# Score copies behind state updates, a plain output for the second block, block sums on VectorE, and rounding spread over the first turns

## Chip, cores, metric

One core of one Trainium2 chip. The metric is the device time of one execution in microseconds (us); "span" is the time between the first and the last instruction in a profiled execution, some 1.7 to 2.0 us less. All executions reported here were in the fast state, so all of them can be compared.

## The reference, cut

```python
def _attn_ref(q, k, v, f_logit):            # (4, 8, 768, 48): batch, heads, tokens, head_dim
    f = 1.0 / (1.0 + np.exp(-f_logit))
    state = np.zeros((B, H, D, D)); y = np.zeros_like(q)
    for t in range(S):
        state = f[:, :, t, :, None] * state + np.einsum('bhd,bhe->bhde', k[:, :, t], v[:, :, t])
        y[:, :, t] = np.einsum('bhd,bhde->bhe', q[:, :, t], state)
    return y

def _moe_ref(x, w_in, w_out):               # 3072 x 384, 384 x 2048, 2048 x 384
    h = x @ w_in
    sp = np.maximum(h, 0.0) + np.log1p(np.exp(-np.abs(h)))
    return (h * erf(sp)) @ w_out
# reference = _moe_ref(x = attention's y as 3072 rows of 384, w_in, w_out)
```

The linear attention runs in 24 chunks of 128 tokens. The weights and the other inputs arrive as 64-bit numbers, which the kernel turns into float32 on the chip; this work on the weights is what "rounding" means below.

## The kernel before, where the change touches it

A chunk passes through stages d (decays: matmul, two exponentials on ScalarE, two multiplies on VectorE), t (transposes), s (scores and state) and y (attention's output). The two engines concerned meet in d and in s:

```python
    def stage_d(g):
        ...
        nc.tensor.matmul(ps, lhsT=tri[:], rhs=lts[blk][:, j, :], start=True, stop=True)
        nc.scalar.activation(out=dp[:, :, 0:D], in_=..., func=AF.Exp, scale=-1.0)
        nc.scalar.activation(out=kd, in_=..., func=AF.Exp)
        ...
        nc.vector.tensor_tensor(out=qd[:, :, 0:D], in0=..., in1=dp[:, :, 0:D], op=ALU.mult)   # waits for ScalarE
        nc.vector.tensor_tensor(out=kd, in0=..., in1=kd, op=ALU.mult)

    def stage_s(g):
        ...   # matmuls into one PSUM tile of two banks: sc (scores), dS (state increments)
        for c in range(2):
            for r in range(2):
                if FIRST <= g < 2 * ADJACENT:          # chunks 3 to 9
                    nc.scalar.copy(out=qA[half(1 - r), r, :, half(c)], in_=sc[half(c), r])
                    ...                                 # causal mask on GpSimd
                    continue
                nc.vector.tensor_tensor(...)            # the other chunks: VectorE copies and masks
        next_state(2 * g, dS)                           # VectorE: 4 small instructions, 2 of them read dS
        if not last:
            late[g] = lambda: next_state(2 * g + 1, dS)  # 4 more, at the next stage t or at y
```

The slots of a turn, in which everything else is placed (cut):

```python
            for s, _ in enumerate(gen):                 # one matmul group of PE per slot
                due += (1 if s < 42 else 0.6 if s < 72 else 0.3) if it == 0 else 0.42 if it == 1 else 0.6
                while due >= 1:
                    weights_step(); due -= 1            # one rounding step, on VectorE
                if at and s == at[0]:
                    ...                                 # a stage of a chunk
                if it + 3 < n_blocks and s == prepare_at:
                    prepare(it + 3, 0, CPB)             # VectorE clamps the gate logits, ScalarE exp, ln
                ...
                if step:
                    act_step()                          # a step of h * erf(softplus(h)), ScalarE and VectorE by turns
                ...
                    sum_step()                          # additions for the block-wise output product
```

The output product is either plain (8 x 4 products of blocks) or block-wise with 7 products in place of 8, which needs sums of blocks of w_out (`sum_w`, 16 additions, on GpSimd) and of the activations, and additions of the results.

## Time and profile before

| | before |
|---|---|
| median of the runs first given | 628.98 us (3 runs, 628.93 to 629.83) |
| span of the profiled run | 627.6 us |
| busy: PE, VectorE (DVE), ScalarE (ACT), GpSimd (POOL) | 94, 75, 61, 6% |
| first hidden matmul, end of turns 0, 1, 2, 3 | 28.2, 105.5, 134.6, 192.4, 250.3 us |
| end of turn 3 to the end of the span | 377.3 us |

The view of instruction groups for 28 to 250 us gives one more reading that matters later. A line holds the operation, its count, after the bar its busy time and the mean ns of one, then the idle time of its engine just before these instructions and what ended it:

```profile
L438 DVE TENSOR_TENSOR sv<-sc,sv 48x192 f32<-48x192 f32 x36 | 12.8, 355 | 7.6 <-ACT qA L488 6.9
...
L488 ACT COPY qA<-sc 64x256 f32<-64x256 f32 x28 | 10.3, 367 | 3.3 <-PE sc L468 2.8
```

VectorE stood 7.6 us before state updates, 6.9 of it for ScalarE's score copies; ScalarE stood only 3.3 us before these copies. The change sets out to remove the first number.

### The profile page before, as it was taken

What the parts mean: (1) busy time and instruction counts of PE and PEld (TensorE: products, weight loads), DVE (VectorE), ACT (ScalarE), POOL (GpSimd) and SP (SyncE); (2) the same over time, 40 slices, a digit from 0 to 9 for tenths busy, and PEclk for the clock granted to TensorE, in tenths of its full rate; (3) what the DMA queues carried; (4) which work ended last, traced back from release to release, by engine and by line L of the source; (5) the groups of instructions that cost most, each with busy time, mean ns of one, the idle gap of its engine ahead of it and who ended that gap; (6) DMA issues with size and microseconds to landing.
All of it is one profiled execution on the core that took longest, in us unless ns stands there. A gap on an engine that the chain in (4) does not pass through costs nothing.

```text
span 627.6 us, 13891 instructions
## 1 busy us (share of the span) xinstructions
PE 589.5 (94%) x5777; PEld 524.7 (84%) x5777; DVE 470.2 (75%) x788; ACT 382.4 (61%) x483; POOL 38.4 (6%) x49
## 2 busy tenths in 40 slices
PE   8788699998976999999999999999999999999995
PEld 7567588887644988988998998998998989989995
DVE  4998998695589778678787876797887694756751
ACT  5725457978864457756675776765775656556200
POOL 1000011010176000000000000000000000000000
PEclk9879799999989899999999999999999999999999
DMA  9997743440321043043052052052030000000000
GB/s 200 247 241 215 216 123 63 88 78 12 63 56 26 1 78 76 1 79 75 4 102 52 2 102 51 3 102 52 3 76 14 2 27 1 19 8 1 25 26 29
DMA packets 155587, 41.35 MB, mean 66 GB/s; under 512 B 147328, under 2 KB 150400, under 8 KB 155520
## 3 DMA queue, kind: packets, MB, share of 16 engines
q1 hardware_dynamic: 153440, 40.02, 29.3%
q8 instruction: 47, 0.77, 0.5%
q10 hardware_dynamic: 2080, 0.39, 0.3%
q14 instruction: 20, 0.16, 0.1%
HBM read 35.59 MB, written 4.72 MB: 64 GB/s over the span
## 4 chain that ended last, share of the span: by engine, by line
PE 72%; DVE 12%; issue 6%; ACT 5%; DMA 2%; SPq 1%; POOL 1%; DVEq 0%; ACTq 0%; POOLq 0%
PE ops L717 31%; PE hps L587 29%; PE y L525 3%; PE ps_t L411 2%; PE ops L670 2%; PE ps_d L380 2%; DVE sv L438 1%; PE sc L460 1%; PE sc L468 1%; DVE sv L439 1%; DVE w_in_sb L322 1%; DMA qn<-in_q_dram 1%; DVE qA L496 1%; DVE w_in_sb L336 1%; ACT L160 1%
## 5 line engine op out<-in xcount | busy, mean ns | idle before, releaser
L587 PE MATMUL hps<-xT,w_in_sb 128*128 128x256 f32 x1152 | 264.7, 386 | 7.8 <-DVE w_in_sb L336 4.4
L587 PEld LDWEIGHTS hps<-xT,w_in_sb 128*128 128x128 f32 x1152 | 218.2, 192 | 41.2 <-DVE w_in_sb L336 3.4
L165 DVE SCALAR_TENSOR_TENSOR e<-x,e 128x1024 f32<-128x1024 f32 x96 | 120.2, 1252 | 13.5 <-ACT x L160 13.2
L160 ACT ACTIVATE x<-Hg,serf_bias 128x1024 f32<-128x1024 f32 x88 | 97.6, 1141 | 0.2
L157 ACT ACTIVATE e<-Hg 128x1024 f32<-128x1024 f32 x44 | 46.6, 1058 | 77.0 <-DVE Hg L561 73.2
L717 PE MATMUL ops<-wT,Hg 128*128 128x192 f32 x352 | 87.6, 331 | 0.0
L717 PE MATMUL ops<-wT,scratch 128*128 128x192 f32 x320 | 76.5, 331 | 5.9 <-DVE scratch L615 5.9
L717 PE MATMUL ops<-w_out_sb,Hg 128*128 128x192 f32 x352 | 72.6, 329 | 0.0
L561 DVE TENSOR_TENSOR Hg<-Hg,e 128x1024 f32<-128x1024 f32 x44 | 54.6, 1240 | 22.5 <-ACT e L559 22.4
L717 PEld LDWEIGHTS ops<-wT,Hg 128*128 128x128 f32 x352 | 62.1, 192 | 2.2
L594 ACT COPY Hg<-hps 128x1024 f32<-128x1024 f32 x44 | 44.4, 1010 | 31.0 <-PE hps L587 30.7
L717 PEld LDWEIGHTS ops<-w_out_sb,Hg 128*128 128x128 f32 x352 | 60.7, 192 | 2.6
L717 PEld LDWEIGHTS ops<-wT,scratch 128*128 128x128 f32 x320 | 57.0, 193 | 6.2 <-issue 6.2
L559 ACT ACTIVATE e<-e 128x1024 f32<-128x1024 f32 x48 | 50.4, 1050 | 6.4 <-DVE e L165 6.3
L496 DVE TENSOR_TENSOR qA<-sc,tri 64x256 f32<-64x256 f32 x68 | 28.7, 422 | 22.3 <-PE sc L468 21.3
L725 DVE TENSOR_TENSOR scratch<-scratch,ops 128x384 f32<-128x384 f32 (+1 forms) x44 | 22.2, 504 | 30.3 <-ACT scratch L733 25.0
L418 ACT COPY qA<-ps_t 64x512 f32<-64x512 f32 x48 | 27.7, 578 | 22.5 <-PE ps_t L411 20.6
L395 DVE TENSOR_TENSOR qd<-qn,dp 128x384 f32<-128x384 f32 x24 | 13.4, 556 | 35.6 <-ACT dp L383 34.4
L717 PE MATMUL ops<-w_out_sb,scratch 128*128 128x192 f32 x160 | 39.5, 328 | 0.0
L525 PEld LDWEIGHTS y<-qA,sv 128*32 128x32 f32 x1536 | 24.6, 113 | 17.2 <-issue 9.2
L525 PE MATMUL y<-qA,sv 128*32 128x64 f32 x1536 | 28.9, 226 | 9.3 <-issue 6.9
L438 DVE TENSOR_TENSOR sv<-sc,sv 48x192 f32<-48x192 f32 x80 | 28.4, 354 | 8.3 <-ACT qA L488 6.9
(109 smaller groups left out, 648.9 us busy)
## 6 DMA issues: line engine op xcount, KB each, us to landing
lt<-in_f_logit_dram SPq DMA_DIRECT2D x24, 192.0 KB, 3.8
qn<-in_q_dram SPq DMA_DIRECT2D x24, 192.0 KB, 3.3
out_dram<-scratch SPq DMA_DIRECT2D x12, 384.0 KB, 2.6
kn<-in_k_dram SPq DMA_DIRECT2D x23, 192.0 KB, 3.5
vt<-in_v_dram SPq DMA_DIRECT2D x23, 192.0 KB, 3.6
sv<-in_v_dram SPq DMA_DIRECT2D x84, 48.0 KB, 2.9
w_out_sb<-in_moe_w_in_dram SPq DMA_DIRECT2D x4, 768.0 KB, 6.3
Hg<-in_moe_w_in_dram SPq DMA_DIRECT2D x4, 768.0 KB, 6.4
```

What stands on the lines that cost most here:

```text
L157: nc.scalar.activation(out=dst[:], in_=h, func=AF.Exp)
L160: nc.scalar.activation(out=dst[:], in_=h, func=AF.Tanh, bias=serf_bias[:, i : i + 1], scale=SERF_KAB[i][0])
L165: nc.vector.scalar_tensor_tensor(out=e[:], in0=x[:], scalar=SERF_KAB[i][2], in1=e[:], op0=ALU.add, op1=ALU.mult)
L418: nc.scalar.copy(out=qAs[g][half(r), r], in_=pss[0][half(r)])
L438: nc.vector.tensor_tensor(out=new, in0=add, in1=old, op=ALU.add)
L496: nc.vector.tensor_tensor(out=qA[half(1 - r), r, :, half(c)], in0=sc[half(c), r], in1=tri1[half(c)].unsqueeze(1).broadcast_to((C, HP, C)), ...
L525: nc.tensor.matmul(y[M * i : M * (i + 1), kt, half(c)], lhsT=sv[:, r, c, a, o : o + M], rhs=qA[:, r, a, half(c)], start=(n == 0), stop=Tru ...
L559: nc.scalar.activation(out=e[:], in_=e[:], func=AF.Tanh, scale=SERF_C)
L561: nc.vector.tensor_tensor(out=h, in0=h, in1=e[:], op=ALU.mult)
L587: nc.tensor.matmul(hps[:, j, :], lhsT=w_in_sb[:, kt, ft * P : (ft + 1) * P], rhs=xTs[blk][:, kt, :], start=(kt == 0), stop=(kt == n_k - 1),)
L594: nc.scalar.copy(out=gr["h"], in_=hps[:])
L717: nc.tensor.matmul(place[n], lhsT=x[:, j, :], rhs=y, start=(gi == 0 and j == 0 and n in first), stop=(gi == n_g - 1 and j == 1), skip_grou ...
```

## The change

Its intent: take VectorE's waits and bunches out of the first turns. Chunks 3 to 9 update the state *before* ScalarE copies the scores. Block 1 gets the plain output product (as block 0 had), so that its sums and additions go. The sums of w_out move from GpSimd to VectorE, and are placed one to every second slot. Rounding and activation steps get a more even pace; the first pieces of the weights are loaded and rounded earlier. The core of the diff:

```diff
+        by_scalar = FIRST <= g < 2 * ADJACENT
+        if by_scalar:
+            next_state(2 * g, dS)
         for c in range(2):
             for r in range(2):
-                if FIRST <= g < 2 * ADJACENT:
+                if by_scalar:
                     nc.scalar.copy(out=qA[half(1 - r), r, :, half(c)], in_=sc[half(c), r])
@@
-        next_state(2 * g, dS)
+        if not by_scalar:
+            next_state(2 * g, dS)
@@ sum_w, four times
-        add(t[:, 0], b12, b11, ALU.subtract, nc.gpsimd)
+        add(t[:, 0], b12, b11, ALU.subtract)
@@ slots(it)
+        if it == 3:
+            return chain(project_first(1), *hiddens(4)), n_ft * CPB + n_h
@@ loads at the start
-        load(1, "qk")
+        load_piece(0)
+        load(1, "qkv")
+        load_piece(1)
         load_f(2)
-        load_piece(0)
-        load(1, "v")
         load(2)
-        load_piece(1)
@@
         stage_t(0)
+        weights_steps(2)
@@ turn 0's places for stages
-                at = [1, 5, 6, 12, 16, 23, 34, 42, 48, 52, 60, 74, 76, 80, 88, 94]
+                at = [1, 5, 8, 12, 16, 23, 36, 43, 48, 52, 60, 74, 76, 80, 88, 94]
@@ rounding
-                due += (1 if s < 42 else 0.6 if s < 72 else 0.3) if it == 0 else 0.42 if it == 1 else 0.6
+                due += (1 if s < 18 else 0.46 if s < 66 else 0.3) if it == 0 else 0.45
@@ activations
-                if it < 2:
-                    step = it == 1 and s % 6 == 3
-                elif it == 2:
-                    step = s % 5 in (1, 3)
+                if it == 0:
+                    step = s >= 24 and s % 8 == 5
+                elif it == 1:
+                    step = s % 5 == 3
+                elif it < 4:
+                    step = s % 7 in (1, 4)
+                elif it == n_blocks - 1:
+                    step = s % 3 == 1
@@ sums
-                    if s == n - 6:
-                        to_sum.extend(sum_h(groups[1, gi]) for gi in range(NS))
-                    sum_step()
+                    if s % 2:
+                        sum_step()
```

(Cut: the places of the sums in memory, the pace of the sums in turn 3, chunk places of turn 2, a prepare ten slots later.)

More of the change, by code (lines that the diff above doesn't have):

```diff
@@ L602, in places @@
         own = [[sums_sb[:, b, n] for n in range(NA)] for b in range(NS)]
-        for _ in range((n_blocks - 3) * n_g // NS):
+        for _ in range((n_blocks - 4) * n_g // NS):
             yield from own
@@ L607, in places @@
             own.insert(0, [x[:, 0 : S_WORDS // (NS * NA)].rearrange("p (j t) -> p j t", j=FG // 2) for x in t])
-        own = own[1::-1] + own[3:] + own[2:3]
+        own = own[1::-1] + own[2:]
         while True:
@@ L612, with add @@
     sum_places = places()
-    def add(out, x, y, op=ALU.add, engine=nc.vector):
-        engine.tensor_tensor(out=out, in0=x, in1=y, op=op)
+    def add(out, x, y, op=ALU.add):
+        nc.vector.tensor_tensor(out=out, in0=x, in1=y, op=op)
     def sum_w(gi):
@@ L621, in sum_w @@
         t = w_sums(gi)
-        add(t[:, 0], b12, b11, ALU.subtract, nc.gpsimd)
+        add(t[:, 0], b12, b11, ALU.subtract)
         yield
-        add(t[:, 1], b22, t[:, 0], ALU.subtract, nc.gpsimd)
+        add(t[:, 1], b22, t[:, 0], ALU.subtract)
         yield
-        add(t[:, 2], b22, b12, ALU.subtract, nc.gpsimd)
+        add(t[:, 2], b22, b12, ALU.subtract)
         yield
-        add(t[:, 3], b21, t[:, 1], ALU.subtract, nc.gpsimd)
+        add(t[:, 3], b21, t[:, 1], ALU.subtract)
     def blocks(h):
@@ L676, in project_first @@
                     if j == FG - 1 and tt == CPB - 1:
-                        to_sum.append(sum_w(gi))
+                        if blk == 0:
+                            to_sum.append(sum_w(gi))
                         if gi == n_g - 1:
@@ L912 @@
             if it == 0:
-                todo = [(stage_s, 2), (stage_y, 2), (stage_d, 3), (stage_t, 3), (stage_s, 3), (stage_y, 3),
+                todo = [(stage_s, 2), (stage_d, 3), (stage_y, 2), (stage_t, 3), (stage_s, 3), (stage_y, 3),
                         (stage_d, 4), (stage_t, 4), (stage_d, 5), (stage_s, 4), (stage_t, 5),
                         (stage_y, 4)] + stages(2)[4:]
-                at = [1, 5, 6, 12, 16, 23, 34, 42, 48, 52, 60, 74, 76, 80, 88, 94]
+                at = [1, 5, 8, 12, 16, 23, 36, 43, 48, 52, 60, 74, 76, 80, 88, 94]
             else:
@@ L920 @@
             if ADJACENT <= it + 2 < n_blocks:
-                at = ([0] if it + 2 == ADJACENT else []) + [2, 26, 42, 54, 76, 90]
+                at = [0, 1, 15, 24, 31, 52, 66] if it + 2 == ADJACENT else [2, 26, 42, 54, 76, 90]
                 at = at[: len(todo)]
@@ L944 @@
                             load_piece(7)
-                if it == 0 and s == 14:
+                if it == 0 and s == 24:
                     prepare(2, 0, CPB)
@@ L963 @@
                 if it == 2:
-                    if s == n - 6:
-                        to_sum.extend(sum_h(groups[1, gi]) for gi in range(NS))
-                    sum_step()
+                    if s % 2:
+                        sum_step()
                 elif it > 2:
-                    if s == n_o and it < n_blocks - 1:
+                    if s == n - n_h and it < n_blocks - 1:
                         to_sum.extend(sum_h(groups[it - 1, gi]) for gi in range(NS))
@@ L972 @@
                         to_sum.extend(sum_h(groups[blk, gi]) for gi in range(NS))
-                    if s < n_o or s % 3 == 0 or it == n_blocks - 1:
+                    if it == 3:
+                        if s % 2:
+                            sum_step()
+                    elif s < n_o or s % 3 == 0 or it == n_blocks - 1:
                         sum_step()
```

## The prediction

> **Names.** The kernel runs twelve turns, one per block of 256 tokens. A turn is a list of slots; one slot is one hidden matmul (L587) or one output matmul (L670, L717). Between slots the program puts attention stages (d, t, s, y of a chunk), rounding steps for the weights (16 pieces of 6 steps, 96 in all) and activation steps (10 per group, a new group every 5). This order fixes what each in-order engine does next.
>
> **What bounds the kernel now.** First the page, parts 1 and 2:
>
> ```profile
> PE 589.5 (94%) x5777; PEld 524.7 (84%) x5777; DVE 470.2 (75%) x788; ACT 382.4 (61%) x483; POOL 38.4 (6%) x49
> ...
> PE   8788699998976999999999999999999999999995
> ...
> POOL 1000011010176000000000000000000000000000
> PEclk9879799999989899999999999999999999999999
> ```
>
> One digit is 15.7 us. PE idles, and its clock drops, only before about 220 us, so only the first turns can give much. I counted hidden matmuls in PE's timeline to find where turns 0 to 5 begin and end, and asked for the windows of these stretches (busy PE, PEld, DVE, ACT, POOL, then granted clock, DMA share, GB/s):
>
> ```profile
> 28.20:105.50 77.30, 67.00 (x736) 55.00 (x736) 71.86 (x119) 36.59 (x60) 5.80 (x8) 0.87 0.70 178
> 105.50:134.60 29.10, 28.69 (x372) 23.88 (x371) 21.68 (x37) 27.04 (x39) 3.15 (x4) 1.00 0.42 72
> 134.60:192.40 57.80, 51.92 (x439) 37.82 (x439) 41.38 (x49) 42.44 (x52) 19.50 (x16) 0.97 0.27 48
> 192.40:250.30 57.90, 50.94 (x533) 46.07 (x532) 47.69 (x80) 33.51 (x39) 6.91 (x7) 0.94 0.24 48
> 250.30:298.10 47.80, 46.82 (x486) 42.57 (x486) 35.77 (x64) 32.78 (x38) 0.00 (x0) 1.00 0.27 52
> 298.10:344.50 46.40, 46.40 (x487) 42.50 (x486) 36.93 (x65) 30.95 (x36) 0.00 (x0) 1.00 0.28 53
> ```
>
> Turn 0 is VectorE's: 72 of 77 us busy, and nearly every piece of the chain between 12 and 72 us is a VectorE instruction, most of them rounding. Turn 5 is the undisturbed kernel, PE without a gap. Turns 2 and 3 carry PE holes beside GpSimd's work. PE's waits name the holes:
>
> ```profile
> PE y L525 <- issue: 6.9, 4, 3.8
> PE ops L717 <- DVE scratch L615: 5.9, 1, 5.9
> PE ps_t L411 <- DVE qd L395: 5.6, 1, 5.6
> PE hps L587 <- DVE w_in_sb L336: 4.4, 2, 3.0
> ```
>
> Last, VectorE's timeline around GpSimd's block sums (172 to 199 us), the same kind of addition during them and after:
>
> ```profile
> 197.95 1.21 DVE L615 TENSOR_TENSOR scratch<-Hg 128x256 f32<-128x256 f32 x1
> ...
> 204.50 0.42 DVE L615 TENSOR_TENSOR scratch<-Hg 128x256 f32<-128x256 f32 x1
> ```
>
> **What the Trainium skill says.** (1) "SBUF — State Buffer", section "Who interferes with whom": a VectorE instruction with two SBUF inputs and a GpSimd instruction that reads SBUF exclude each other for a whole instruction. The trace agrees: 0.42 us becomes 1.21 us. (2) "PSUM — Partial Sum Buffer", section "PSUM bank collisions raise a hardware error": two engines in one bank have to be ordered by software, reads included. The trace agrees: state updates (L438) wait for ScalarE's score copies (L488), 8.6 us in 4 waits, although both only read the score tile. (3) "TensorE: Matmul & The Clock Gate", Part 1: an idle window of about 3.4 us halves PE's clock, and it comes back after about as long a busy one. The trace agrees roughly: after the 5.6 us hole at 66.6 us the clock is 0.55 in 72 to 76 us, and after the hole that ends at 203 us pairs of output matmuls run at 0.64 us in place of 0.325. So a hole of 5 us costs near 7.
>
> **The change part by part.**
>
> *Plain output for block 1.* From the chain: 32 L717 records take 5.20 us, so 0.1625 each (a float32 matmul is two records). Block-wise: 56 x 2 x 0.1625 = 18.2 us. Plain: 32 matmuls of twice the columns, an estimate of 32 x 2 x 0.325 = 20.8 us. PE pays **+2.6 us**. In return, block 1's 16 additions (16 x 0.43 = 6.9 us of VectorE) and 4 evictions (2.2 us) go, and with them the 5.9 us wait on its sums at the start of turn 3.
>
> *Block sums of w_out on VectorE.* 16 additions of 128x384 at about 0.55 us (the duration of L395, same shape): +8.8 us of VectorE. Gone is the mutual exclusion: adding up what VectorE's instructions from 172 to 199 us take beyond their usual durations gives about 9.7 us. A wash in busy time, but it is spread over turns 2 and 3, and the mask for y of chunk 8 no longer queues behind these sums (the 3.8 us hole that ends at 178 us).
>
> *Rounding spread.* Six steps of a piece take 0.56 + 0.56 + 0.96 + 0.56 + 0.96 + 0.96 = 4.55 us, 0.79 a step with gaps. When qd of chunk 4 is due, the old order has emitted 10 + 35 = 45 steps, the new one 12 + 18 + 0.46 x 19 = 38 or 39: 6.5 x 0.79 = 5 us less VectorE work in front of it. In turn 0 this is path: the 5.6 us hole ends by that qd.
>
> *Loads and the start.* Piece 0 now comes ahead of chunk 1's loads and its first steps ahead of d of chunk 1. At the 220 GB/s of the first windows piece 0 lands near 10 us; f of chunk 2 comes behind two pieces, near 15 us. I count 1 to 2 us of new stalls, mostly regained as the rounding is further on: the first hidden matmul at 29.5 instead of 28.3.
>
> *State updates first.* VectorE loses 8.6 us of waiting, but ScalarE's copies now wait for a VectorE that is behind. For y of chunk 3 I work out copies at 54.9 to 56.4 us (before: 52.6 to 54.2), so this y comes 1 us later than before, with a hole in front of it.
>
> *Turn 0* then: slot 24 near 59 us (before 57.5), t of chunk 4 near 67.5 without a wait (before 72.2, then half clock), the rest limited by PE as before: **it ends near 99.8 instead of 105.5.**
>
> *Turn 1*: VectorE gets 21.6 steps x 0.79 = 17, attention 9 and activations 7 = 33 us against 28 of PE. From 55 us to the end of turn 2 I sum 53 (rounding) + 30 (attention) + 27 (activations) + 6 (sums) = 116 us of VectorE in some 122: 95%. It keeps up, barely, and I allow 1 us here and 1.5 in turn 2. Turn 1 takes 29, ending at 128.8.
>
> *Turn 2*: 96 hidden records 20.7 (from the chain), plain 20.8, stages 7 (turn 5: 46.4 - 18.2 - 20.7 = 7.5) = 48.5, with the allowance 49.7, ending at **178.5 (before 192.4)**. Activations are further on (33 steps when the first plain output starts, 10 needed), so no forced bunch.
>
> *Turn 3*: 20.8 + 20.7 + 8 (one more s) = 49.5, with waits 50: **228.5 (before 250.3)**. Turn 4 stays at 47.8, and from 298.1 to the end 329.5 us stay as they are, since PE has no gap there. Sum: 228.5 + 47.8 + 329.5 = 605.8 us of span; the median before is 1.4 us over its span, so **607 us**.
>
> **The rivals.**
> *VectorE is the bound and stays it.* It was 93% busy in turn 0; total work hardly falls. Holes would move from t of chunk 4 into turns 1 and 2, where rounding now lies beside activations. For it: the 95% above, with dependency stalls of some 5% seen between 72 and 144 us. Against: turn 1 before had 7 us free. Then the end of turn 2 is at 184 or later: 612 to 618 us.
> *ScalarE becomes hostage to VectorE.* Copies of scores wait for updates at the end of VectorE's queue, and evictions of hidden groups queue behind them; two buffers give 5 us of grace. Each such wait costs PE up to 4 us and the clock. For it: y of chunk 3 above. Against: from turn 1 VectorE is hardly behind. 610 to 615 us.
> *The start slips.* Moved loads stall d of chunk 1 and the prepare of chunk 2 by more than I count: up to +4 us, 611 us.
> *All holes close.* Turns 0 to 3 at their content: turn 0 near 95, then 28, 48 and 49: 598 us.
>
> **Range and chances.** The holes of turns 2 and 3 (5.9 and 3.8 us, plus the half clock behind each, plus contention) have causes that the diff plainly removes: 10 to 15 us after paying 2.6. Turn 0 gives 3 to 10. The 2% line is at 616.4, a gain of 12.6; only if turn 0 gives nothing and turns 1 and 2 show new holes is it missed. Predicted 607 us, 80% range 600 to 616; faster by over 2%: 0.87, within: 0.11, slower: 0.02.
>
> **What would show it right or wrong.** Right: PE's waits without L717 on L615 and without the 5.6 us on qd; no GpSimd sums, L615 at 0.42 to 0.55 us throughout; VectorE no longer waiting for L488; turn boundaries near 100, 129, 178 and 228; turn 5 at 46.4. Wrong: new PE waits on qd, state or masks in turns 1 and 2 with VectorE over 95% busy there (first rival); ScalarE waiting for L438 or L439 by many us with PE waiting for L594 (second); the first hidden matmul after 32 us (third); or a steady turn other than 46.4.

## The result

628.69 us median of 4 runs (627.44 to 629.04) against 629.17 us of before (4 runs, 628.93 to 629.83). The ratio is 0.9987 with a 95% interval of 0.997 to 1.0004: no change. Ratios here are the mean time of one kernel's fast runs over that of the other's of the same rounds, so not quite the ratio of the medians quoted. I had predicted 607 and gave "within 2%" a chance of 0.11.

The page of the changed kernel, parts 1 and 2 (busy time per engine; then digits per slice of 15.7 us):

```profile
PE 591.9 (94%) x5729; PEld 517.7 (83%) x5729; DVE 461.2 (74%) x784; ACT 384.6 (61%) x485; POOL 16.6 (3%) x33
...
PE   7695999879899999999999999999999999999995
...
POOL 1001011100100000000000000000000000000000
PEclk9978899898999999999999999999999999999998
```

GpSimd has lost its sums, as intended. PE's gaps have moved to the left: slices 4, 8 and 9 (47 to 63 us, 110 to 141 us) where before the largest lay at 63 to 78 us and at 173 to 204 us. The windows of turns 0 to 5 (stretch, length, then busy PE, PEld, DVE, ACT, POOL, granted clock, DMA share, GB/s):

```profile
29.70:105.30 75.60, 67.93 (x736) 55.21 (x736) 62.89 (x104) 44.89 (x67) 6.56 (x8) 0.87 0.68 179
105.30:145.90 40.60, 32.87 (x372) 27.21 (x372) 30.17 (x47) 27.16 (x40) 3.39 (x4) 0.87 0.33 57
145.90:199.00 53.10, 50.08 (x440) 36.61 (x439) 42.93 (x65) 36.74 (x47) 3.41 (x4) 1.00 0.27 48
199.00:249.00 50.00, 50.00 (x486) 37.18 (x485) 38.22 (x65) 37.04 (x42) 0.51 (x2) 1.00 0.26 53
249.00:295.50 46.50, 46.50 (x486) 42.59 (x485) 37.46 (x66) 30.63 (x36) 0.00 (x0) 1.00 0.28 53
295.50:341.90 46.40, 46.40 (x486) 42.50 (x485) 37.23 (x66) 32.85 (x39) 0.00 (x0) 1.00 0.28 53
```

Turn 1 is the surprise: 40.6 us where before took 29.1 and I predicted 29.0. In turns 0 and 1 the granted clock is 0.87. Turns 2 to 4 gain 4.7, 7.9 and 1.3 us; turn 0 gains 1.7 in place of 7; turn 1 loses 11.5. That is where the gain went: not hidden, but spent again in turn 1 and at the start (1.5 us). PE's waits:

```profile
PE y L528 <- POOL qA L493: 8.5, 3, 4.3
PE y L528 <- issue: 6.3, 4, 3.1
...
PE ps_t L411 <- DVE qd L395: 0.8, 1, 0.8
```

The waits that were predicted to go are gone (5.9 us on the block sums; qd fell from 5.6 to 0.8). New ones hold y, the product that needs the copied and masked scores. The groups in 28 to 250 us, to be laid beside those of before:

```profile
L438 DVE TENSOR_TENSOR sv<-sc,sv 48x192 f32<-48x192 f32 x37 | 13.1, 355 | 2.0 <-ACT qA L490 1.2
...
L490 ACT COPY qA<-sc 64x256 f32<-64x256 f32 x28 | 10.3, 367 | 26.6 <-DVE sv L438 11.6 <-DVE sv L439 8.2 <-DVE sv L436 5.3
```

VectorE's wait fell from 7.6 to 2.0 us. ScalarE's, before the same 28 copies, rose from 3.3 to 26.6. How one of these waits comes about is seen in the three engines' timelines of turn 1 (start, duration, instruction, in brackets the idle time before it and what ended it). ScalarE:

```profile
130.06 0.51 ACT L383 ACTIVATE dp<-ps_d 128x384 f32<-128x384 f32 x1
130.43 0.52 ACT L386 ACTIVATE kd<-ps_d 128x384 f32<-128x384 f32 x1
136.21 1.51 ACT L490 COPY qA<-sc 64x256 f32<-64x256 f32 x4 [5.26 <-DVE sv L438]
...
140.37 1.02 ACT L597 COPY Hg<-hps 128x1024 f32<-128x1024 f32 x1
```

VectorE in the same stretch:

```profile
130.60 0.56 DVE L395 TENSOR_TENSOR qd<-qn,dp 128x384 f32<-128x384 f32 x1 [2.39 <-ACT dp L383]
131.07 0.55 DVE L399 TENSOR_TENSOR kd<-kn,kd 128x384 f32<-128x384 f32 x1
...
132.61 1.22 DVE L564 TENSOR_TENSOR wT<-wT,e 128x1024 f32<-128x1024 f32 x1
133.74 1.22 DVE L165 SCALAR_TENSOR_TENSOR e<-x,e 128x1024 f32<-128x1024 f32 x1
134.99 0.35 DVE L438 TENSOR_TENSOR sv<-sc,sv 48x192 f32<-48x192 f32 x1
```

And PE:

```profile
139.97 1.30 PE L528 MATMUL y<-qA,sv 128*32 128x64 f32 x38 [3.73 <-POOL qA L493]
```

Read it as a chain. VectorE stands at qd until ScalarE's exponential dp is there (2.39 us). Both engines then go on together, but ScalarE's next instructions are the score copies, and these may not read the tile until VectorE's state updates have. VectorE has six other instructions queued ahead of those (qd, kd, two rounding steps, two activation steps), 4.4 us from 130.60 to 134.99. So ScalarE stands for 5.26 us, and everything behind the copies comes later: the mask on GpSimd, then in ScalarE's own queue the transposes' copies and the eviction of a hidden group at 140.37. PE runs out and waits 3.73 us at y. Then VectorE in turn arrives early at the next qd: its waits for dp in 55 to 199 us are 21.0 us in the changed kernel, 4.8 us (55 to 192 us) before. Two in-order queues stand for each other by turns. The Trainium skill, "TensorE: Matmul & The Clock Gate", in its table at the top and Part 1, calls the queues of ScalarE and VectorE strict first-in, first-out; the trace agrees: nothing in ScalarE's queue ran in those 5.26 us, although PE had finished at 133.2 us the transposes that ScalarE was to copy.

Chunk by chunk (3 to 9), ScalarE's waits before these copies are 8.2, 3.4, 0, 5.3, 5.3, 3.0 and 1.2 us, so the chain above, chunk 7's, is not the only case. The longest, chunk 3's, comes about otherwise: VectorE waits for nobody there, but works off rounding steps without a gap from 47.7 to 53.9 us before it gets to the updates. There it is late by its load.

### The profile page after: what moved, and what is told of

Read it like the earlier page. It is cut to its first block, busy times and chain, and to the rows that moved or that the text cites. A ratio compares the mean times of both kernels' runs of the same rounds, so it can differ in the third digit from the quotient of the medians.

```text
span 627.3 us, 13755 instructions
## 1 busy us (share of the span) xinstructions
PE 591.9 (94%) x5729; PEld 517.7 (83%) x5729; DVE 461.2 (74%) x784; ACT 384.6 (61%) x485; POOL 16.6 (3%) x33
## 4 chain that ended last, share of the span: by engine, by line
PE 71%; DVE 12%; ACT 7%; SPq 3%; DMA 3%; issue 2%; POOL 0%; ACTq 0%; DVEq 0%
PE hps L590 30%; PE ops L721 25%; PE ops L673 7%; PE y L528 3%; PE ps_t L411 2%; PE ps_d L380 2%; DVE sv L438 1%; PE sc L468 1%; PE sc L460 1%; ACT x L160 1%; SPq L391 1%; DVE sv L439 1%; DVE qA L498 1%; DVE Hg L564 1%; DVE e L165 1%
## 5 line engine op out<-in xcount | busy, mean ns | idle before, releaser
L590 PE MATMUL hps<-xT,w_in_sb 128*128 128x256 f32 x1152 | 269.5, 391 | 5.6 <-ACT xT L532 2.0
L590 PEld LDWEIGHTS hps<-xT,w_in_sb 128*128 128x128 f32 x1152 | 221.5, 195 | 41.2 <-ACT xT L532 2.8
L165 DVE SCALAR_TENSOR_TENSOR e<-x,e 128x1024 f32<-128x1024 f32 x96 | 117.1, 1220 | 17.0 <-ACT x L160 16.5
L721 PE MATMUL ops<-wT,Hg 128*128 128x192 f32 x320 | 78.9, 328 | 0.0
L721 PE MATMUL ops<-wT,scratch 128*128 128x192 f32 x288 | 67.8, 326 | 0.9 <-DVE scratch L729 0.9
L721 PE MATMUL ops<-w_out_sb,Hg 128*128 128x192 f32 x320 | 65.1, 326 | 0.0
L721 PEld LDWEIGHTS ops<-wT,Hg 128*128 128x128 f32 x320 | 55.8, 190 | 1.9
L721 PEld LDWEIGHTS ops<-w_out_sb,Hg 128*128 128x128 f32 x320 | 54.6, 190 | 2.0
L721 PEld LDWEIGHTS ops<-wT,scratch 128*128 128x128 f32 x288 | 50.3, 190 | 1.1 <-issue 1.1
L498 DVE TENSOR_TENSOR qA<-sc,tri 64x256 f32<-64x256 f32 x68 | 28.7, 422 | 28.3 <-PE sc L468 27.4
L721 PE MATMUL ops<-w_out_sb,scratch 128*128 128x192 f32 x144 | 35.2, 326 | 0.0
```

The costliest lines, as they stand in the source:

```text
L165: nc.vector.scalar_tensor_tensor(out=e[:], in0=x[:], scalar=SERF_KAB[i][2], in1=e[:], op0=ALU.add, op1=ALU.mult)
L498: nc.vector.tensor_tensor(out=qA[half(1 - r), r, :, half(c)], in0=sc[half(c), r], in1=tri1[half(c)].unsqueeze(1).broadcast_to((C, HP, C)), ...
L590: nc.tensor.matmul(hps[:, j, :], lhsT=w_in_sb[:, kt, ft * P : (ft + 1) * P], rhs=xTs[blk][:, kt, :], start=(kt == 0), stop=(kt == n_k - 1),)
L721: nc.tensor.matmul(place[n], lhsT=x[:, j, :], rhs=y, start=(gi == 0 and j == 0 and n in first), stop=(gi == n_g - 1 and j == 1), skip_grou ...
```

## The experiments

15 kernels, all correct within the tolerance. Theory: the swap of state updates and score copies ate the gain. Rivals: VectorE's amount of work, the activation pace, the new start. Against the kernel before, only runs 13 and 15 are faster by a clear 2%; runs 7, 9 and 12 lie at that line.

### 1. The changed kernel, swap undone

```diff
-        if by_scalar:
-            next_state(2 * g, dS)
...
-        if not by_scalar:
-            next_state(2 * g, dS)
+        next_state(2 * g, dS)
```

> The changed kernel with one part undone: state updates again behind ScalarE's score copies. Theory A (ScalarE held by VectorE): in the changed kernel ScalarE stood 25 us in turns 0 and 1 waiting for state updates (8.2 + 3.4 + 5.3 + 5.3 + 3.0), and PE lost 11.6 us in turn 1 on the masks behind those copies. With the order undone turn 1 falls from 40.6 to about 30 us and the time to 612 to 618 us. Theory B (turn 1 has too much VectorE work, whatever the order): turn 1 stays at 38 us or more, VectorE waits for ScalarE in place of the reverse, time 625 to 630 us.

618.98 us (617.82 to 619.16, 4 runs), ratio to before 0.9836 (0.9817 to 0.9856), span 616.1. Against the changed kernel this is 9.7 us; it lies 1 us above the range of theory A (612 to 618) and far from that of B. The same place of the program in ScalarE's timeline:

```profile
121.83 0.50 ACT L386 ACTIVATE kd<-ps_d 128x384 f32<-128x384 f32 x1
122.36 1.52 ACT L488 COPY qA<-sc 64x256 f32<-64x256 f32 x4
```

The copies follow the exponentials at once; VectorE's row of instructions from qd to the state update is even longer than in the changed kernel (5.3 us, 121.99 to 127.28) and does not hold up the copies. Turn 0 ends at 99.5 us, as predicted (99.8). Turns 1 and 2 take 32.3 and 55.8 us, 9.4 us more than predicted, turn 3 takes 50.0 as predicted. So the swap is one half of the miss, and something in turns 1 and 2 is the other.

### 2. The kernel before, swap alone

```diff
+        if by_scalar:
+            next_state(2 * g, dS)
         ...                                   # copies
-        next_state(2 * g, dS)
+        if not by_scalar:
+            next_state(2 * g, dS)
```

> The kernel before with only the swap: state updates ahead of the score copies. Theory A: VectorE is most behind in turn 0 here (93% busy), so ScalarE is held at chunks 3 to 7 and the time rises by 3 to 12 us, to 632 to 641 us. Theory B: the swap by itself is neutral or a small gain (8.6 us of VectorE waits gone), 624 to 630 us.

630.71 us (629.22 to 633.34, 20 runs), ratio 1.0025 (1.0013 to 1.0036). It costs 1.5 us here, in place of the 9.7 us in the changed kernel; the time lies between the ranges of the two theories. ScalarE stands before the copies of chunks 3 to 9 here too (1.0, 6.9, 4.0, 1.8, 3.1, 0 and 1.2 us), so its waits do not turn into time one for one. PE's y waits appear here as well (3.2 us on the mask at 55 us, 2.1 at 133 us), and turn 2 ends 3 us later than before, but at 205 us the wait on GpSimd's block sums has shrunk (5.2 us for 5.9). That this wait takes up a part of the loss is argued, not shown; why turn 1 itself loses less here is open (run 4 points to the old activation pace, which this kernel has).

### 3. The changed kernel, score tile split in two

The tile of two banks becomes two tiles of one bank, so that state updates and copies order each other bank by bank; two copies go ahead, then the update, then two copies.

```diff
-        ps = ps_sc.tile([P, 2, 512], FP32, name="sc", tag="sc")
+        pss = [ps_sc.tile([P, 512], FP32, name=f"sc{i}", tag=f"sc{i}") for i in range(2)]
@@
-        if by_scalar:
-            next_state(2 * g, dS)
-        for c in range(2):
-            for r in range(2):
+        for n in range(4):
+                c, r = (n % 2, n // 2) if by_scalar else (n // 2, n % 2)
+                if by_scalar and n == 2:
+                    next_state(2 * g, dS)
```

> The changed kernel with the score tile split into two tiles of one bank each, and per chunk the two copies of bank 0, then the state update (which reads bank 0), then the two copies of bank 1. ScalarE then never waits for the first state update, and VectorE waits for two copies in place of four. Theory A: at least as fast as e1, 608 to 616 us. Theory B: as the changed kernel, 625 to 630 us.

619.73 us (619.07 to 620.95), ratio 0.9852 (0.9828 to 0.9876). ScalarE no longer has a wait on sv among its large ones. The time equals that of the swap undone, and is more than theory A's 608 to 616: it is enough that ScalarE need not stand for VectorE, and no gain of the finer order beyond that is shown.

### 4. The changed kernel, old activation pace in turns 0 and 1

```diff
-                    step = s >= 24 and s % 8 == 5
+                    step = False
                 elif it == 1:
-                    step = s % 5 == 3
+                    step = s % 6 == 3
```

> The changed kernel with the old activation pace in turns 0 and 1 (none in turn 0, every sixth slot in turn 1), all else as changed. Theory B: this takes about 6 activation instructions of VectorE (7 us) and two table loads of ScalarE out of turn 1, so turn 1 falls to 33 us or less and the time to 619 to 623 us. Theory A: the wait of the copies for VectorE remains at chunks 3, 6 and 7; turn 1 stays above 35 us, time 622 to 630 us.

638.71 us (637.5 to 640.31), ratio 1.0143 (1.012 to 1.0165): slower than both. Neither theory's number was met. PE's waits say why:

```profile
PE ops L673 <- DVE wT L564: 7.3, 1, 7.3
...
PE ops L673 <- DVE Hg L564: 4.6, 1, 4.6
```

With the old pace and the other new parts, the plain output products wait for activations, 11.9 us. So the new activation pace is a needed part of the change. But the run shows more: turn 1, with the swap in place, took only 33.5 us (104.4 to 137.9) in place of 40.6, near theory B's 33. At chunk 7 one activation step less stands in VectorE's row between qd and the first state update, and ScalarE's wait is shorter:

```profile
126.00 0.56 DVE L395 TENSOR_TENSOR qd<-qn,dp 128x384 f32<-128x384 f32 x1 [5.85 <-ACT dp L383]
...
129.14 0.35 DVE L438 TENSOR_TENSOR sv<-sc,sv 48x192 f32<-48x192 f32 x1
```

```profile
130.35 1.51 ACT L490 COPY qA<-sc 64x256 f32<-64x256 f32 x4 [4.00 <-DVE sv L438]
```

The row takes 3.14 us for 4.39 and the wait 4.00 us for 5.26, some 1.25 us less each. Turn 1's loss needs the swap (run 1: 32.3 us without it) and the new activation pace together.

### 5. Swap undone, rounding earlier in turn 0

```diff
-                due += (1 if s < 18 else 0.46 if s < 66 else 0.3) if it == 0 else 0.45
+                due += (1 if s < 18 else 0.46 if s < 36 else 0.65) if it == 0 else 0.45
```

> e1 (changed, swap undone) with the rounding pace of turn 0 raised from slot 36 on (0.65 of a step per slot in place of 0.46 and 0.3), so that about 16 steps (12 us of VectorE) move out of turns 1 and 2. Theory C (what is left over my estimate in e1, turn 1 at 32.3 and turn 2 at 55.6 us, is VectorE running without a gap from 122 to 160 us on rounding plus activations): turn 2 falls to 51 us or less, turn 0 grows by 0 to 3 us, time 612 to 617 us. Theory D (it is the chain of one activation after another between ScalarE and VectorE): within 1.5 us of e1, 617 to 621 us.

618.19 us (618.0 to 621.47), ratio 0.9844 (0.981 to 0.9878): as without, which is theory D's number. Turns 1 and 2 take 84.5 us for 88.1 of run 1, but turn 0 ends 4.4 us later (103.9), so the end of turn 2 is again near 188 us. VectorE's work was moved, not made less.

### 6. Swap undone, sums of w_out on GpSimd at the new places

```diff
-        add(t[:, 0], b12, b11, ALU.subtract)
+        add(t[:, 0], b12, b11, ALU.subtract, nc.gpsimd)      # and three more
```

> e1 with the block sums of w_out on GpSimd again, at the new places of the program. If the exclusion between GpSimd and VectorE was worth what I read from the trace of before (9.7 us of stretched VectorE instructions and a 3.8 us hole of PE), this is slower than e1 by 3 to 8 us, 622 to 627 us; if spreading the sums alone did it, within 1.5 us of e1.

618.16 us (617.61 to 619.42), ratio 0.9834 (0.9811 to 0.9857): no difference to run 1. The second number of the expectation was met, but not for its reason, as the sums are no more spread in time than before. Of the 16 on GpSimd, the first and the last:

```profile
170.80 0.99 POOL L615 TENSOR_TENSOR wT<-w_out_sb 128x384 f32<-128x384 f32 x1
...
191.61 1.00 POOL L615 TENSOR_TENSOR wT<-w_out_sb,wT 128x384 f32<-128x384 f32 x1
```

In the kernel before they lay at 172.1 to 198.9 us, in the changed one, on VectorE, at 185.7 to 206.6 us. VectorE's instructions beside them are stretched as before (2.02 us for 1.22), but PE's only wait there is 0.26 us, at y.

### 7. Swap undone, old start

Run 1 with the old load order and without the two early rounding steps.

```diff
-        load_piece(0)
-        load(1, "qkv")
-        load_piece(1)
+        load(1, "qk")
         load_f(2)
+        load_piece(0)
+        load(1, "v")
         load(2)
+        load_piece(1)
@@
         stage_t(0)
-        weights_steps(2)
```

> e1 with the old order of loads and the old first rounding steps. In e1 the first hidden matmul begins at 29.7 us, before at 28.3. If the start moved only the same VectorE work about, the time stays within 1.5 us of e1 (617 to 620.5); if the new start costs its 1.4 us, 616.5 to 618; if it is needed for the pieces of turn 0, 620 to 624 us.

616.75 us (615.78 to 620.91), ratio 0.9827 (0.9784 to 0.9869). The first hidden matmul is at 28.3 us again, 1.4 earlier. The medians say 2.2 us, but the intervals overlap: that the new start costs anything is not shown.

### 8. The kernel before, sums of w_out on VectorE

The four edits of run 6 the other way round, in the kernel before and nothing else.

> The kernel before with only the 16 block sums of w_out moved from GpSimd to VectorE, at the old places. Gone: 9.7 us of stretched VectorE instructions and the mask queued behind the sums (3.8 us of PE); added: 8.8 us on VectorE at the time when it is nearly full (190 to 200 us). I expect 621 to 627 us; if the sums only change engines, 628 to 631 us.

621.47 us (620.52 to 622.25), ratio 0.9881 (0.9857 to 0.9905): 7.6 us of gain by this alone. The wait on block sums fell from 5.9 to 2.7 us, that of y at 175 us from 3.8 to 1.5. So GpSimd's sums hurt in the kernel before and not in run 6, though they run in one bunch both times. What differs is what stands beside them: block 1's own sums on VectorE, for which PE waited 5.9 us, are gone in run 6. That this decides it is argued, not tested.

### 9. Old start and swap undone, the two multiplies of d four slots later

From here on run 7 is the base. VectorE gets qd and kd four slots after ScalarE's exponentials, so that it need not stand for them.

```diff
+        multiplies.append([wait_slots[0], g, kd, dp])    # run 4 slots later, or at stage t
+        if not wait_slots[0]:
+            multiply()
```

> Made from the run with the swap undone and the old start (616.75 us, 0.983 of before): VectorE's two multiplies of d (qd and kd) are emitted four slots later than ScalarE's two exponentials, so that VectorE works on other things while ScalarE gets to them. Theory (what is left over the prediction in turns 1 and 2 is mostly stalls of a VectorE that stands at qd for ScalarE, 11.5 us between 55 and 186 us): these stalls fall below 5 us, turns 1 and 2 lose some 4 of their 86.7 us, total near 613. Rival (VectorE has the stalls to spare, PE is held up by the order of the two engines' queues around y and the pieces): the stalls go and the time stays within 1.5 us of 616.75. A third outcome: t then waits for qd, PE gets waits on qd of over 3 us and the run is slower than 617.

616.15 us (614.84 to 617.67), ratio 0.9807 (0.9782 to 0.9833). VectorE's stalls at qd fell from 11.5 to 3.7 us, and the time hardly: the rival's outcome. Turns 1 and 2 take 84.1 us for 86.7 of run 7, but turn 0 ends 2.6 us later.

### 10. The changed kernel, swap from chunk 4 on only

```diff
-        if by_scalar:
+        state_first = by_scalar and g > FIRST
+        if state_first:
             next_state(2 * g, dS)
```

> The changed kernel, but at chunk 3 (the one of the seven chunks concerned that falls in turn 0's first 25 slots) the state updates stand behind the score copies again; chunks 4 to 9 keep the new order. Theory (each chunk whose copies wait for state updates costs on its own, chunk 3 the 4.3 us hole and the half clock behind it): turn 0 ends at 99 to 100.5 us in place of 105.3, turns 1 and 2 still take 6 or more us over those of the run with the whole swap undone, total 622 to 625. Rival (the loss at chunk 3 starts a lag that the later ones only inherit): turns 1 and 2 come back too, total 618 to 620. If the early loss only moves to the later waits (slack given back), turn 2 still ends near 199 and the total stays at 627 to 629.

624.93 us (624.2 to 625.17), ratio 0.9938 (0.9922 to 0.9955), where the theory put it (622 to 625). Chunk 3's hole of 4.3 us is one of 1.8 us again, as in run 1, and turn 0 ends at 101.4 us, a little later than expected; turn 1 still takes 39.6. So the later swapped chunks do not inherit a lag from the first: by the medians chunk 3 costs 3.8 us and the other six 5.9. A caution on lengths from one profile: behind this same hole of 1.8 us the clock was 0.50 from 55.5 to 62.2 us here and stayed at 1.00 in run 1, and 26 hidden records took 8.15 us for 5.88.

### 11. Run 7 with the old activation pace in the last turn

```diff
-                elif it == n_blocks - 1:
-                    step = s % 3 == 1
```

> Made from the run with the swap undone and the old start: only the last turn's activation pace is the old one again. In the changed kernel the last stretch took 101.3 us where the kernel before took 100.1, which I had not predicted. If the new pace in the last turn is the cause, the last stretch is 100.1 again and the time 1.2 us less, near 615.5; if it comes from elsewhere (the state in which block 10 leaves the queues), nothing moves.

618.08 us (617.14 to 619.26), ratio 0.9837 (0.982 to 0.9854): nothing gained. Where the last 1 to 2 us of the end come from is open.

### 12. Run 7 with the clamp earlier

In run 7, ScalarE stands at the exponential of the gate logits for a clamp that VectorE has queued last, and PE then stands for a hidden group's eviction. ScalarE in turn 2 of run 7:

```profile
153.25 0.84 ACT L364 ACTIVATE lt<-lt 128x768 f32<-128x768 f32 x1 [3.33 <-DVE lt L360]
```

PE at that place:

```profile
156.06 0.70 PE L587 MATMUL hps<-xT,w_in_sb 128*128 128x256 f32 x2 [2.90 <-ACT Hg L594]
```

It is the same pattern as the swap's, with another pair of instructions.

```diff
+                if it + 3 < n_blocks and s == max(0, prepare_at - 12):
+                    clamp(it + 3)                          # VectorE's part alone
                 if it + 3 < n_blocks and s == prepare_at:
-                    prepare(it + 3, 0, CPB)
+                    prepare(it + 3, 0, CPB, True)          # ScalarE's part alone
```

> Made from the run with the swap undone and the old start (616.75 us, 0.983): VectorE's clamp of the gate logits (L360) of a block is emitted 12 slots (6 for block 2) before ScalarE's exponential that reads it, in place of in the same slot. In that run ScalarE stands at this exponential for the clamp at the end of VectorE's queue, 3.8, 3.5 and 3.3 us, and the last of these makes the eviction of a hidden group late: PE stands 2.9 us at 156 us. Theory (what is left over the prediction in turns 1 and 2 comes from such places, where ScalarE stands for what VectorE has queued last, as in the swap but by another pair of instructions): ScalarE's waits at the exponential fall below 3 us in all, PE's 2.9 us hole on the eviction goes, turns 1 and 2 take 83 to 84 us in place of 86.7, total 613 to 614.5, ratio near 0.977. Rival (VectorE has too much work there, whatever the order): the wait goes elsewhere (activation, y) and the time stays within 1 us of 616.75, ratio 0.981 to 0.984.

615.55 us (614.21 to 617.55, 5 runs), ratio 0.9797 (0.9772 to 0.9821). The waits at the exponential after 31 us are gone and so is PE's hole of 2.90 us; turns 1 and 2 take 84.1 us for 86.7, about as the theory had it. But turn 0, in which two of the clamps were moved as well, ends 1.8 us later (100.9 us at a clock of 0.91), and the time is 1.2 us less, between the two expectations. As in run 9, a wait went, and most of it was given back elsewhere.

### 13. Run 7 with less of VectorE's rounding

For w_out's eight pieces the last three of six VectorE steps are left out (the result is slightly wrong on purpose, still within the tolerance): by count 14.9 us less VectorE work in turns 1 and 2 (in the windows, 16.3 us less than in run 7), everything else in place.

```diff
+        if i >= n_pieces:
+            yield
+            yield
+            return
```

> Made from the run with the swap undone and the old start (616.75 us, 0.983). For the eight pieces of w_out the last three of the six VectorE steps of rounding (0.56 + 0.96 + 0.96 = 2.48 us) are left out and their slots stay empty: w_out keeps only the upper half of its digits, a slightly wrong result on purpose. Six of these pieces lie in turns 1 and 2: 14.9 us less VectorE work there, 5 in turn 0. Theory A (the amount of VectorE's work holds turns 1 and 2): they take 78 to 81 us in place of 86.7 (78.7 predicted), turn 0 loses 1 to 2 us too, total 608 to 610, ratio near 0.97. Theory B (the order in which ScalarE and VectorE meet, or PE's own work, holds them): 84 to 87 us, total 613 to 616.

610.74 us (607.9 to 611.16, 5 runs), ratio 0.9726 (0.971 to 0.9743); the profiled run is the fastest of them, span 606.2. Its windows of turns 1 and 2 (columns as above):

```profile
99.60:127.80 28.20, 28.17 (x370) 23.54 (x370) 19.20 (x33) 25.56 (x38) 3.80 (x4) 1.00 0.42 74
127.80:177.50 49.70, 49.70 (x440) 36.69 (x439) 39.57 (x61) 38.34 (x50) 3.00 (x4) 1.00 0.31 56
```

PE has no gap, and the turns take 28.2 and 49.7 us: 77.9, predicted 78.7. Theory A holds: less work for VectorE is enough to close what was left in turns 1 and 2. That nothing but the amount of work could close it does not follow; see run 15.

### 14. The changed kernel with less rounding

The same edit with the swap in place.

> The changed kernel, swap in place, with the same steps of w_out's rounding left out (slightly wrong on purpose). Theory A (the swap costs what VectorE is behind when a score tile is ready): with 15 us less work in turns 1 and 2 ScalarE's waits at the score copies of chunks 4 to 9 fall from some 17 us to under 9, turns 1 and 2 take 84 to 88 us in place of 93.7, chunk 3's hole in turn 0 stays (no w_out piece lies before it), total 619 to 622, so 8 to 12 us over the run without the swap shrink to some 10 in turn 0 plus 2. Theory B (the swap ties the engines together whatever the load): the waits at the copies stay at 15 us or more and the time within 4 us of 628.

626.78 us (625.0 to 628.12, 13 runs), ratio 0.9967 (0.9955 to 0.9979). My theory for this one (A) failed. ScalarE's waits in 55 to 197 us:

```profile
ACT qA L494 <- DVE sv L442: 11.0, 3, 5.3
ACT qA L494 <- DVE sv L443: 8.4, 1, 8.4
```

And its window of turn 1:

```profile
104.20:143.90 39.70, 31.22 (x370) 25.68 (x370) 22.54 (x37) 27.10 (x40) 2.81 (x4) 0.91 0.33 58
```

VectorE is busy 22.5 of 39.7 us in turn 1, and ScalarE stands for it all the same. The second line is chunk 3's wait, in turn 0, where the edit takes nothing out of VectorE's way; it says nothing about load. For chunks 4 to 9 ScalarE's waits at the copies, whoever the profile names for them, add up to 16.9 us, against 18.0 in the changed kernel, with 14.8 us less VectorE work in the windows of turns 1 and 2. With less rounding the swap costs 16 us (626.78 against 610.74, of which 2.2 may be the start), more than with all of it. So in turns 1 and 2 the swap does not cost because VectorE is overloaded. At chunk 7 the row from qd to the first state update is untouched by the edit (the same six instructions, 4.39 us), it starts only when ScalarE's dp ends, and the wait is 5.26 us as in the changed kernel. Run 4 took an instruction out of that very row, and there the wait did shrink.

### 15. Runs 9 and 12 together

> Multiplies of d four slots later and the clamp 12 slots earlier in one kernel (616.15 and 615.55 us alone, 616.75 without either). If both waits each take 1 to 2 us, 613 to 614.5, ratio near 0.977; if VectorE's amount of work holds turns 1 and 2, 615 to 616.5 as each alone.

612.37 us (611.83 to 614.33, 4 runs), ratio 0.9745 (0.9729 to 0.9761). Each edit alone gave 0.6 and 1.2 us in medians, within the noise; together they give 4.4, a little more than was expected. Turns 1 and 2 take 81.3 us now; turn 0 of the profiled run, the slowest of the four, takes 76.1 us at a clock of 0.85, so that turn 2 ends at 185.5 us, as in run 7 (185.8). Where the three faster runs gained is thus not shown, nor why the two edits do more together than each alone. This is the fastest version that rounds in full, 2.5% under before and 2.6% under the changed kernel (612.37 over 628.69).

### All in one table

Lengths in us, from profiled runs; the span is the sum of a column.

| | before | predicted | changed | 1 swap undone | 7 + old start | 10 swap from chunk 4 | 13 less rounding | 14 swap, less rounding |
|---|---|---|---|---|---|---|---|---|
| to the first hidden matmul | 28.2 | 29.5 | 29.7 | 29.7 | 28.3 | 29.4 | 27.4 | 29.1 |
| turn 0 | 77.3 | 70.3 | 75.6 | 69.8 | 70.8 | 72.0 | 72.2 | 75.1 |
| turn 1 | 29.1 | 29.0 | 40.6 | 32.3 | 32.5 | 39.6 | 28.2 | 39.7 |
| turn 2 | 57.8 | 49.7 | 53.1 | 55.8 | 54.2 | 53.5 | 49.7 | 53.1 |
| turn 3 | 57.9 | 50.0 | 50.0 | 50.0 | 49.9 | 49.8 | 49.5 | 49.2 |
| turn 4 to the end | 377.3 | 377.3 | 378.3 | 378.5 | 378.4 | 378.7 | 379.2 | 378.6 |
| span | 627.6 | 605.8 | 627.3 | 616.1 | 614.1 | 623.0 | 606.2 | 624.8 |

## Why the prediction was wrong, step by step

The predicted span was 605.8, the measured 627.3, so 21.5 us are to be explained. Two steps carry them: the swap 11.2 us (627.3 to 616.1 of run 1; 9.7 by the medians), and turns 1 and 2 of run 1 9.4 us (88.1 to 78.7). The rest of the column adds up to 0.9.

*State updates first: the step that failed.* It said that "VectorE loses 8.6 us of waiting" and that y of chunk 3 comes 1 us later. The first half came true at the updates (7.6 to 2.0 us in the groups, a wait that did not bind), but VectorE's waits at qd rose from 4.8 to 21.0 us. The time of the copies was close: worked out 54.9 to 56.4 us, measured 55.5 to 57.0. What failed is the price. The hole in front of y was named, but the sum gave it 1.5 us (slot 24 near 59 for 57.5): this y began 3.0 us later than before (57.51 for 54.53) behind a hole of 4.3 us, slot 24 at 60.9, and the clock was 0.50 until 66.7 us (26 hidden records in 8.76 us, 5.88 in run 1). And nothing at all was set down for the other six chunks, which cost 5.9 us by the medians (run 10). The second rival described the mechanism almost as it is and was put aside with "from turn 1 VectorE is hardly behind". For turn 1 runs 4 and 14 show that argument to be wrong in kind, not only in size: it needs no VectorE that is behind by its load, only a row of instructions between its wait for ScalarE and the updates that ScalarE waits for. At chunk 3 VectorE was behind by its load, as the rival said. The rival's 610 to 615 us was still too low, as it counted the waits beside an otherwise fulfilled plan.

*Turns 1 and 2: a mis-sized term.* That VectorE "keeps up, barely", with 1 and 1.5 us allowed, was the first rival's ground. Without the swap (run 1) the turns ran 3.3 and 6.1 us over the plan, allowances included, and the end of turn 2 is at 187.6, in that rival's "184 or later". Runs 5, 9 and 12 removed a bunch or a wait each, took 2.6 to 3.6 us out of turns 1 and 2, gave 1.8 to 4.4 of it back in turn 0 and won 0.6 to 1.2 us in the medians; run 13 took 14.9 us of work away and turned 86.7 us into 77.9. The work itself was not set too low: the prediction summed 116 us of VectorE from 55 us to the end of turn 2, and the windows show it busy 111.2 us there in run 1. The mis-sized term is its standing: 116 in 122 us is 95%, run 1 reached 84% (111.2 of 132.6 us), and in run 7 VectorE stood 11.5 us at qd and 4.0 us before state updates, both times for ScalarE. By its time, run 15 shows that order counts as well, once two stalls are taken away together.

*Rounding spread and turn 0: right.* The wait of t on qd went from 5.6 to 0.8 us, and turn 0 ends at 99.5 us in run 1, 99.8 predicted.

*Plain output for block 1: right in length.* Turn 3 takes 50.0 us as predicted, and the wait of 5.9 us on its sums is gone.

*Block sums: right for this kernel, for a partly wrong reason.* With the swap undone the engine does not matter (run 6; "A wash in busy time"). But in the kernel before the engine alone was worth 7.6 us (run 8), and "spread over turns 2 and 3" came to 185.7 to 206.6 us in the changed kernel, no wider than the 172.1 to 198.9 us before. One reading was wrong, too: the mask before the hole that ends at 178 us is chunk 9's and did not queue behind the sums; it ran at 170.57 us, the first sum at 172.11. The last state update for this y, on VectorE, ended only at 177.4 us.

*The start: right,* 29.7 for 29.5. That it was "mostly regained" is not shown: by the medians the old start is 2.2 us better, within the noise.

*After turn 3: 1.0 us off.* Turn 4 is 1.3 us shorter and the last turns 2.3 us longer than I took over; run 11 rules out the last turn's activation pace.

*Small slips in the sums.* 48.5 and an allowance of 1.5 make 50.0 us for turn 2, not 49.7; six steps make 4.56 us, not 4.55; and 1.4 us between time and span mixes two executions (1.7 in the profiled one, 629.27 and 627.6). They change nothing here.

*Range and chances.* I wrote that the 2% line is missed "only if turn 0 gives nothing and turns 1 and 2 show new holes". Turn 0 gave 1.7 us and turn 1 showed holes. The condition was right; the mistake was to give it a chance of 0.13 with the cause of both lying in one line of the diff.

## What to carry to other kernels

When a change reverses which of two in-order engines goes first on shared data, do not ask which wait disappears but what stands in the other engine's queue between its own last wait for its partner and the instruction now waited for: that stretch (4.4 us at chunk 7) sets the new wait, and less work elsewhere in that engine's queue need not shorten it. Work it out at each occurrence: over seven chunks the wait came to between 0 and 8.2 us. An engine that copies for PE, like ScalarE here, should not stand for one that is off PE's path. And where a plan needs an engine busy for 95% of a stretch while it takes its inputs from another in-order engine, expect less (84% here), and take away work in an experiment before moving it about; moving it three times told less than removing it once.

## What the Trainium skill lacked or had wrong

- "PSUM — Partial Sum Buffer", section "PSUM bank collisions raise a hardware error": it says that reads of one bank by two engines have to be ordered, and not that the choice of the order has a price. Here it was 3.3 us of ScalarE's waiting one way (kernel before) and 26.6 us the other (changed kernel); undoing the order there gave 9.7 us, while in the kernel before it cost 1.5 us.
- "TensorE: Matmul & The Clock Gate", Part 1 and the table at the top: strict first-in, first-out queues are stated, and no page tells what two such queues do that wait for each other by turns. Here ScalarE stood 5.26 us and VectorE 2.39 us in one round, and less work elsewhere in VectorE's queue did not shorten it (5.26 us again in run 14), one instruction less between the two waits did (4.00 us in run 4).
- The same page, Part 1, has the clock halve after at least one idle window of about 3.4 us: in the changed kernel a PE hole of 3.13 us that ends at 120.08 us was already followed by half clock (0.50 in 121.4 to 124.8 us), and in the hole that begins at 136.2 us the clock went from 1.00 to 0.50 at 138.5 us, some 2.2 us in. How much of a window must be idle is not stated there.
- "SBUF — State Buffer", section "Who interferes with whom": the exclusion of VectorE and GpSimd is right (1.22 us becomes 2.02 in run 6), but the page cannot tell what it weighs: 7.6 us for 16 additions in one bunch in the kernel before (run 8), nothing measurable for the same 16, again in one bunch, in run 6.
